# Windowed attention and a squared-ReLU layer on one core: another planned order, and 128-row turns of x for groups 1 to 4

## The chip, the cores and the metric

The kernel runs on one core of one Trainium2 chip. The metric is device time in microseconds of one execution, shown as the median of the timed runs. A profiled execution gives the trace; its span runs from the first to the last instruction.

The engines are named as in the profile: PE is TensorE's matmuls, PEld its loads of weights, DVE is VectorE, ACT ScalarE, POOL GpSimd and SP SyncE. SP does no arithmetic here and only issues DMAs.

## What is computed

Attention in a window of 32 positions to each side, over 8 batches of 8 heads, 576 positions and 64 channels; its result, laid out as 4608 tokens of 512 channels, goes through two matmuls with a squared ReLU between them.

```python
def _attn_ref(q, k, v):                       # each (8, 8, 576, 64)
    scores = (1 / np.sqrt(64)) * np.matmul(q, k.transpose(0, 1, 3, 2))
    mask = np.abs(pos[:, None] - pos[None, :]) <= 32
    scores = np.where(mask, scores, -1e9)
    attn = np.exp(scores - max); attn = attn / (attn.sum(-1) + 1e-9)
    return np.matmul(attn, v)

def _moe_ref(x, w_in, w_out):                 # (4608, 512), (512, 2048), (2048, 512)
    r = np.maximum(x @ w_in, 0.0)
    return (r * r) @ w_out

x = attn_out.transpose(0, 2, 1, 3).reshape(4608, 512)
```

## The kernel before

**Attention, in 24 groups.** A group is 192 positions of one batch with all 8 heads, three groups to a batch; group `G` is `g = G % 3` of batch `b = G // 3`. For each group GpSimd issues loads of q, k and v, which also turn float32 into bfloat16 (`load_qk` at L487, `load_v` at L536; `load_pair` at L519 in batches 0 and 1). Then q and k are turned so that channels lie on partitions: for groups 0 to 5 by matmuls with the identity (`turn_pe`, L578) and an eviction (L606, L609), from group 6 on by DMA transposes on SP (`turn_dma`, L618, four for a group, called `td` in the code).

The scores `S` are L659 in groups 0 to 2 and L707 after that, 24 matmuls with 64 rows. ScalarE takes the exponential (`X`, L721 and L724), VectorE multiplies with the band mask (`M`, L729 and L735), which gives `pt`. Two value products follow, `P{G}A` and `P{G}B` (L763, eight matmuls each). v has a column of ones, so each product also gives the row sums. After the first, VectorE takes the reciprocal (`R`, L782) and multiplies (`N`, L785), which gives 64 rows of x in `xa`; then the place in PSUM is cleared (`Z`, L793 on ScalarE or L795 on VectorE), since the second product adds onto it, and the same steps give 128 rows in `xb`. The 64 rows of `xa` lie on partitions 64 to 127.

**Turning x** (`xturn`). x is needed with channels on partitions, in the ring `xt`. Groups 0 to 4 are turned on TensorE: `T{G}a` turns the 64 rows of `xa` by four transposes of 64 rows (L843), `T{G}b` the 128 rows of `xb` by four of 128 (L848), both into one PSUM bank, and ScalarE evicts both at once (L860). Group 0 has its own code (L813, L818). From group 5 on, two DMA transposes on SP do it (L864, L867).

**The two matmuls.** The up-product `A` (L889) takes blocks of 192 tokens up to token 2304 and of 256 after that, in pieces of eight matmuls. ScalarE applies the ReLU (`r`, L895), and ScalarE or VectorE squares (`g`, L905 or L903) into the ring `gt`. The last 512 tokens go through seven products in place of eight (`mm1_pair`, L966). The down-product runs over pairs of 128 tokens, seven products `P1` to `P7` of eight matmuls each (`mm2_pair`, L1083, with sums formed by VectorE at L1069); the first two blocks go without that (`mm2`, L1023).

**What sets the order.** `Prog.rec` records every operation with its reads and writes, a duration, and a key, which is a place in the order that the code wishes for. `Prog.schedule` then plans time with these numbers: at each step the engine that is free first takes the ready operation with the smallest key, and some may go to either ScalarE or VectorE (`alt`). Keys get random offsets from `SEEDS` within `NOISE`, and offsets for each kind of operation (`OFFS`, `FLEX`). A DMA's planned landing is that of a model of the queues plus a slack: `LSLACK` for loads from batch 2 on, `XSLACK` for turns of x on SP. The plan only fixes the order on each engine; on the chip every operation waits for semaphores. `gate` holds the loads of a group back until a given operation on TensorE is done, from group 12 on the second value product of group `G - 4`. `kind` and `change` charge the plan about 0.1 us where TensorE changes between matmuls of 64 rows and others, and prefer to keep such operations together. Where the plan leaves TensorE free in the opening, matmuls over zeros (L412, "idle") are put in.

```python
def kind(self, op):
    n = op.name
    return "s" if n[0] == "S" or n[0] == "T" and n[-1] == "a" else ...
def change(self, a, b):
    return 0 if a == b else 110 if b == "s" else 100 if a == "s" or b == "t" else 30 if b == "v" else 0
```

## Time and profile before

| what | us |
|---|---|
| median of 3 timed runs | 290.09 |
| the three runs | 293.07, 290.09, 288.38 |
| the profiled execution's own time | 291.74 |
| its span, first to last instruction | 289.9 |
| TensorE busy in the span | 282.1 |
| VectorE / ScalarE / GpSimd busy | 219.8 / 215.4 / 106.8 |

In the rows of the profile the form `128*128 128x256` means 128 rows of weights by 128 columns, and an output of 128 partitions by 256. `xN` is the number of instructions. In the order of time a row begins with start and length in us; the start of the next row is the better measure of how long a stretch of matmuls holds TensorE, since matmuls overlap at their ends. `[0.74 <-DMA xt<-xb]` behind a row is idle time of that engine ahead of it and what ended it.

### The profile page before, as it was taken

To read this page: it belongs to the slowest core of one execution; us is meant where nothing else is said; L and a number is where in the kernel's file an instruction comes from. 1 tells how busy PE (TensorE), PEld (TensorE's weight loads), DVE (VectorE), ACT (ScalarE), POOL (GpSimd) and SP (SyncE) were. 2 spreads that over 40 slices of the span, in tenths; PEclk is the share of its full clock that TensorE was granted. 3 is DMA by queue.
4 is the path that set the end of the run, shared out by engine and by line. 5 is a ranking of instruction groups with operands and counts; after the bars stand their busy time and mean duration, and the time that the engine had idled before them with its cause. 6 is when DMAs were issued, how large, how long until landed. Compare 5 with 4: busy or idle time off the path is not lost.

```text
span 289.9 us, 8460 instructions
## 1 busy us (share of the span) xinstructions
PE 282.1 (97%) x3424; PEld 245.2 (85%) x3430; DVE 219.8 (76%) x472; ACT 215.4 (74%) x404; POOL 106.8 (37%) x143
## 2 busy tenths in 40 slices
PE   7998999999999999999999899999999999999996
PEld 2567988698899999999988788898889888888885
DVE  6668679969668978688866664987898857889863
ACT  3379999985489889688978898777887855788310
POOL 8985663260264664454665246425000000000000
PEclk9999999999999999999999999999999999999999
DMA  9999999999599999999999999999922030202124
GB/s 167 188 194 176 205 179 161 135 195 132 128 158 179 131 165 141 210 150 134 179 145 188 150 122 186 169 152 187 170 41 84 20 102 0 76 0 76 72 75 145
DMA packets 158983, 39.59 MB, mean 137 GB/s; under 512 B 148320, under 2 KB 154592, under 8 KB 158944
## 3 DMA queue, kind: packets, MB, share of 16 engines
q0 software_dynamic: 106016, 17.93, 89.8%
q1 hardware_dynamic: 47888, 12.07, 31.7%
q10 hardware_dynamic: 5040, 9.05, 10.0%
q8 instruction: 27, 0.44, 0.7%
q14 instruction: 12, 0.10, 0.1%
HBM read 36.70 MB, written 9.44 MB: 159 GB/s over the span
## 4 chain that ended last, share of the span: by engine, by line
PE 87%; DMA 5%; DVE 5%; ACT 2%; issue 1%; DVEq 0%
PE ht L889 32%; PE outp L1083 29%; PE at L1083 6%; PE at L763 4%; DMA xt<-xb 3%; PE at L707 3%; PE outp L1023 2%; PE at L966 2%; PE ht L966 2%; DMA oe<-in_q_dram 1%; PE outp L412 1%; PE outp L889 1%; PE at L889 1%; DVE kt L609 1%; PE at L578 1%
## 5 line engine op out<-in xcount | busy, mean ns | idle before, releaser
L889 PE MATMUL ht<-xt,w 128*128 128x192 bf16 (+1 forms) x1120 | 119.5, 256 | 0.7 <-DMA xt<-xb 0.7
L889 PEld LDWEIGHTS ht<-xt,w 128*128 128x128 bf16 x1120 | 96.6, 98 | 8.0 <-DMA xt<-xb 1.0
L895 ACT ACTIVATE rt<-ht 128x384 bf16<-128x384 f32 (+1 forms) x140 | 72.2, 529 | 21.7 <-PE ht L889 20.6
L905 ACT ACTIVATE gt<-rt 128x384 bf16<-128x384 bf16 (+1 forms) x122 | 67.1, 566 | 2.4
L536 POOL DMA_DIRECT2D v<-in_v_dram x48 | 38.3, 805 | 43.8 <-PE at L763 19.4
L487 POOL DMA_DIRECT2D kraw<-in_k_dram x36 | 28.1, 783 | 36.5 <-issue 14.6
L487 POOL DMA_DIRECT2D qraw<-in_q_dram x36 | 28.1, 782 | 10.3 <-PE ht L889 5.2
L1083 PE MATMUL outp<-w,gt 128*128 128x256 bf16 x224 | 29.0, 273 | 0.0
L1083 PE MATMUL outp<-tw,gt 128*128 128x256 bf16 x224 | 29.0, 273 | 0.0
L1083 PE MATMUL outp<-tw,ss 128*128 128x256 bf16 x224 | 28.9, 273 | 0.1
L1083 PEld LDWEIGHTS outp<-w,gt 128*128 128x128 bf16 x224 | 21.5, 98 | 2.6
L1083 PEld LDWEIGHTS outp<-tw,gt 128*128 128x128 bf16 x224 | 21.7, 98 | 2.3
L1083 PEld LDWEIGHTS outp<-tw,ss 128*128 128x128 bf16 x224 | 21.2, 98 | 2.7 <-DVE ss L1069 0.3
L721 ACT ACTIVATE e<-at 128x1024 bf16<-128x1024 f32 x21 | 21.4, 1021 | 2.1 <-PE at L707 1.9
L763 PE MATMUL at<-v,pt 128*128 128x66 bf16 x384 | 20.1, 194 | 0.5 <-DVE pt L735 0.5
L735 DVE TENSOR_TENSOR pt<-em,mask 64x512 bf16<-64x512 bf16 x42 | 17.6, 420 | 3.8 <-ACT em L724 2.4
L763 PEld LDWEIGHTS at<-v,pt 128*128 128x128 bf16 x384 | 17.9, 98 | 1.7 <-DVE pt L735 0.8
L903 DVE TENSOR_TENSOR gt<-rt 128x384 bf16<-128x384 bf16 (+1 forms) x30 | 11.4, 382 | 10.2 <-ACT rt L895 10.0
L729 DVE TENSOR_TENSOR pt<-e,mask 128x1024 bf16<-128x1024 bf16 x21 | 14.5, 691 | 5.4 <-ACT e L721 5.0
L1103 DVE TENSOR_TENSOR oe<-outp,uu 128x256 f32<-128x256 f32 (+1 forms) x28 | 15.4, 551 | 3.4 <-PE outp L1083 2.8
L785 DVE TENSOR_TENSOR xa<-at,rs 64x512 bf16<-64x512 f32 x24 | 16.7, 695 | 1.1
L785 DVE TENSOR_TENSOR xb<-at,rs 128x512 bf16<-128x512 f32 x24 | 16.5, 686 | 0.7
(151 smaller groups left out, 412.0 us busy)
## 6 DMA issues: line engine op xcount, KB each, us to landing
out_dram<-oe ACTq DMA_DIRECT2D x34, 256.0 KB, 4.6
qraw<-in_q_dram POOLq DMA_DIRECT2D x36, 96.0 KB, 7.3
w<-in_moe_w_in_dram POOLq DMA_DIRECT2D x4, 512.0 KB, 11.0
v<-in_v_dram POOLq DMA_DIRECT2D x16, 128.0 KB, 8.1
w<-in_moe_w_out_dram POOLq DMA_DIRECT2D x4, 512.0 KB, 17.6
v<-in_v_dram POOLq DMA_DIRECT2D x16, 96.0 KB, 7.3
kraw<-in_k_dram POOLq DMA_DIRECT2D x12, 112.0 KB, 7.2
kraw<-in_k_dram POOLq DMA_DIRECT2D x12, 96.0 KB, 7.4
```

The costliest lines, as they stand in the source:

```text
L487: self.p.rec("POOL", lambda e, j=j: e.dma_start(raw[0:h, j, :].rearrange("p (h d) -> p h d", h=8), s[:, j]), writes=[("raw", t, G % NRAW, ...
L536: self.p.rec("POOL", lambda e, j=j, lo=lo, hi=hi, k0=k0: e.dma_start(vt[lo - k0:hi - k0, j, :, 0:64], self.v[b, :, lo:hi, :].rearrange("h ...
L721: self.p.rec("ACT", lambda e: e.activation(e2[:], self.AT[:, 0:1024], ACTF.Exp, scale=0.125), reads=lo, writes=[("e", n)], key=key, dur=ac ...
L729: self.p.rec("DVE", lambda e: e.tensor_tensor(out, e2[:].rearrange("p (h s q) -> p h s q", h=8, s=2), mb, ALU.mult), reads=[("e", n), ("ma ...
L735: self.p.rec("DVE", lambda e, w=w, r=r, x=x, mm=mm: e.tensor_tensor(pt[x:x + 64, w, :, 0:64], e1[r:r + 64, :].rearrange("p (h q) -> p h q" ...
L763: mm = e.matmul(avp[:, c:c + VS], pt[:, 4 * (h % 2) + h // 2, :], vt[:, w, h, :], start=(w == 0 and y == 0), stop=True, skip_group_check=True)
L785: self.p.rec("DVE", lambda e: e.tensor_tensor(x[r0:128, :].rearrange("p (x y c) -> p x y c", x=2, y=4), av[:, :, :, 0:64], rb, ALU.mult), ...
L889: mm = e.matmul(ht[:, n * x:n * x + n], self.W1[:, ft, 128 * d:128 * d + 128], self.XT[:, ft, r:r + n], start=(ft == 0), stop=(ft == 3))
L895: self.p.rec("ACT", lambda e: e.activation(rt[:, 0:c], ht[:, 0:c], ACTF.Relu), reads=htag, writes=[("rt", k % 4)], key=key, dur=act(c), na ...
L905: alt=("ACT", lambda e: e.activation(gt[:, d0:d0 + len(ds), r:r + n], rr, ACTF.Square), act(c), "g")
L1083: mm = e.matmul(op[:, 256 * half:256 * half + 256], a[:, d, :], w[:, d, :], start=first and d == 0, stop=d == 7, skip_group_check=True)
L1103: self.p.rec("DVE", lambda e: e.tensor_tensor(out, src, other, ALU.add), reads=btags[bank] + rd, writes=wr, key=key + k * PSTEP - DLEAD, d ...
```

## The change

Three things change in the program. First, the planner's numbers: more slack for turns of x on SP (3200 to 4200 ns) and for loads (1200 to 1600 ns), other seeds with more noise, other offsets of keys, down-products later (`LAGP`), and two entries of the opening's list of loads exchanged. Second, `T1a` to `T4a`: the transposes of `xa` take all 128 rows of it, of which the first 64 are zeros, and write 128 columns; `T{G}b` and the eviction shift by 64 columns. Third, three operations fill the zero rows of the three `xa` buffers once, at the head of the program. The planner no longer counts `T1a` to `T4a` among the 64-row matmuls. `KPL` and `LAGS` are 0, so the code that they bring stays unused.

```diff
-XSLACK = 3200
-LSLACK = 1200
+XSLACK = 4200
+LSLACK = 1600
-NOISE = 0.1
+NOISE = 0.4
-LAGP = 14.0
+LAGP = 15
+TFULL = True
...
-        return "s" if n[0] == "S" or n[0] == "T" and n[-1] == "a" else ...
+        return "s" if n[0] == "S" or n[0] == "T" and n[-1] == "a" and (not TFULL or n == "T0a") else ...
...
+            c = 64 * TFULL
             def f0(e):
                 for j in range(4):
-                    mm = e.transpose(ps[:, 192 * j:192 * j + 64], xa[64:128, 128 * j:128 * j + 128], self.ID[64:128, 64:128])
+                    mm = e.transpose(ps[:, 192 * j:192 * j + 128], xa[:, 128 * j:128 * j + 128], self.ID[:])
             def f1(e):
                 for j in range(4):
-                    mm = e.transpose(pb[:, 192 * j + 64:192 * j + 192], xb[:, 128 * j:128 * j + 128], self.ID[:])
+                    mm = e.transpose(pb[:, 192 * j + 64 + c:192 * j + 192 + c], xb[:, 128 * j:128 * j + 128], self.ID[:])
...
-            self.p.rec("PE", f0, reads=[("xa", G % 3), "id"], writes=bank, key=key, dur=110, name=f"T{G}a")
+            self.p.rec("PE", f0, reads=[("xa", G % 3), "id"] + [("xz", G % 3)] * TFULL, writes=bank, key=key, dur=110, name=f"T{G}a")
...
-                                                     ps[:, 0:768].rearrange("p (j q) -> p j q", j=4), ACTF.Copy),
+                                                     ps[:, c:768 + c].rearrange("p (j q) -> p j q", j=4), ACTF.Copy),
...
+        for i in range(3 * TFULL):
+            x = self.XA[i][0:64, :]
+            at(-20, lambda i, x: self.p.rec("DVE", lambda e: e.memset(x, 0.0), reads=["zz"], writes=[("xz", i)], key=XZKEY + i, dur=200, name=f"xz{i}",
+                                            alt=("ACT", lambda e: e.activation(x, self.ZZ[0:64, :], ACTF.Copy), 490, "Z")), i, x)
```

The new order on the engines shows at three places. A row is a run of equal instructions; `at` is the PSUM tensor of attention, `ht` that of the up-product, `outp` that of the down-product.

The first place is TensorE around the turn of x of group 1. Before, from its second value product (first row):

```order
L763 MATMUL at<-v,pt 128x66 x8
L659 MATMUL at<-qt,kt 128x128 x8
L889 MATMUL ht<-xt,w 128x192 x8
L843 MATMUL at<-ident,xa 128x64 x4
L848 MATMUL at<-ident,xb 128x128 x4
L889 MATMUL ht<-xt,w 128x192 x8
```

The same place in the changed kernel, whose lines have moved (L767 for L763, L663 for L659, L898 for L889, L850 and L857 for the turns):

```order
L767 MATMUL at<-v,pt 128x66 x8
L663 MATMUL at<-qt,kt 128x128 x8
L850 MATMUL at<-ident,xa 128x128 x4
L857 MATMUL at<-ident,xb 128x128 x4
L898 MATMUL ht<-xt,w 128x192 x16
```

Both turns have moved ahead of an up-product piece that used to stand before them.

The second place is TensorE between the two value products of group 6. Before, with L763 at both:

```order
L763 MATMUL at<-v,pt 128x66 x8
L1083 MATMUL outp<-w,gt 128x256 x8
L1083 MATMUL outp<-tw,ss 128x256 x16
L1083 MATMUL outp<-tw,gt 128x256 x8
L763 MATMUL at<-v,pt 128x66 x8
```

And in the changed kernel, where L767 is the value product and L1092 the down-product:

```order
L1092 MATMUL outp<-tw,ss 128x256 x16
L767 MATMUL at<-v,pt 128x66 x8
L1092 MATMUL outp<-tw,gt 128x256 x8
L1092 MATMUL outp<-w,gt 128x256 x8
L767 MATMUL at<-v,pt 128x66 x8
```

Four products of the down-product stood between them, and two stand there now.

The third place is TensorE in groups 7 and 8, from the first value product of group 7 to that of group 8 (the third L763); L707 are the scores of group 8. Before:

```order
L763 MATMUL at<-v,pt 128x66 x8
L889 MATMUL ht<-xt,w 128x192 x16
L1083 MATMUL outp<-w,gt 128x256 x8
L889 MATMUL ht<-xt,w 128x192 x8
L763 MATMUL at<-v,pt 128x66 x8
L889 MATMUL ht<-xt,w 128x192 x16
L707 MATMUL at<-qt,kt 128x64 x24
L889 MATMUL ht<-xt,w 128x192 x16
L1083 MATMUL outp<-tw,ss 128x256 x8
L889 MATMUL ht<-xt,w 128x192 x16
L763 MATMUL at<-v,pt 128x66 x8
```

In the changed kernel, L711 being the scores:

```order
L767 MATMUL at<-v,pt 128x66 x8
L898 MATMUL ht<-xt,w 128x192 x24
L767 MATMUL at<-v,pt 128x66 x8
L898 MATMUL ht<-xt,w 128x192 x16
L711 MATMUL at<-qt,kt 128x64 x24
L898 MATMUL ht<-xt,w 128x192 x24
L767 MATMUL at<-v,pt 128x66 x8
```

Between the two value products of group 7 the same three up-product pieces stand without the down-product among them; between the scores and the first value product of group 8 stand three pieces, where four and a down-product were.

More of the change, by code (lines that the diff above doesn't have):

```diff
@@ L29 @@
 GD = 3
-GK = 7.0
+GK = 6.5
 TDKEY = 5.0
@@ L35 @@
 TBK = 0
+TFULL = True
+XZKEY = -5
+LAGS = 0.0
+KPL = 0
 GDL = 1
@@ L161, in kind @@
         n = op.name
-        return "s" if n[0] == "S" or n[0] == "T" and n[-1] == "a" else "t" if n[0] == "t" else "v" if n[0] == "P" and "." not in n else ""
+        return "s" if n[0] == "S" or n[0] == "T" and n[-1] == "a" and (not TFULL or n == "T0a") else "t" if n[0] == "t" else "v" if n[0] == "P" and "." not in n else ""
     def change(self, a, b):
@@ L1242, in build @@
                 at(t0 / 64 - 2, self.mm1_tile, t0, t0 / 64 + MOE)
-                for d in range(8):
-                    at(t0 / 64 + d + MOE, self.mm1_pair, t0, d, t0 / 64 + d + MOE)
+                for y in range(2):
+                    for d in range(0, KPL, 2):
+                        for d0 in (d, 8 + d):
+                            key = t0 / 64 + d / 2 - 2 + 0.2 * (d0 > 7) + MOE if y == 0 else t0 / 64 + 8 - KPL / 2 + d / 2 + 0.2 * (d0 > 7) + MOE
+                            at(key, self.mm1, t0 + 256 * y, 256, [d0, d0 + 1], key)
+                for d in range(KPL, 8):
+                    key = t0 / 64 + d - KPL / 2 + MOE
+                    at(key, self.mm1_pair, t0, d, key)
                 t0 += 512
```

25 lines of the change are left out of this document (14 added, 11 removed), and 2 rows, old and new, of the table OPENING.

## The prediction

> **What bounds the kernel now.** I read the page first, for the share of each engine and for the groups of instructions, then the list of TensorE's waits, then the order of time on TensorE.
>
> ```profile
> span 289.9 us, 8460 instructions
> PE 282.1 (97%) x3424; PEld 245.2 (85%) x3430; DVE 219.8 (76%) x472; ACT 215.4 (74%) x404; POOL 106.8 (37%) x143
> ```
>
> The program has one core, and its TensorE (PE) computes for 282.1 of 289.9 us. The other engines have about a quarter of their time free. A gain can only come from TensorE's list itself or from its 7.8 us without work. These are told by two more views: the list of what TensorE waited for, with total, count and longest in us, and a table by stage.
>
> ```profile
> PE at L843 <- DVE xb L785: 0.8, 1, 0.8
> PE ht L889 <- DMA xt<-xb: 0.7, 1, 0.7
> ...
> PE at L763 <- DVE pt L735: 0.5, 1, 0.5
> ...
> 0.00:2.00 2.00, 0.81 (x2) 0.28 (x3) 1.14 (x9) 1.25 (x1) 1.02 (x6) 1.00 0.03 10
> 2.00:30.00 28.00, 25.77 (x283) 16.82 (x284) 20.20 (x57) 17.30 (x29) 22.69 (x30) 1.00 1.60 194
> ...
> 287.00:290.00 3.00, 0.14 (x2) 0.00 (x0) 0.52 (x2) 0.00 (x0) 0.00 (x0) 0.97 0.59 206
> ```
>
> The first column of a stage after its length is TensorE's busy time, and the third number from the end the granted clock, which is full. Of the 7.8 us, 1.2 lie ahead of the first matmul, 2.2 in the opening up to 30 us, 2.8 behind the last matmul. In the 257 us between there are only two waits worth a name, 0.7 us on a turned block of x (`DMA xt<-xb`) and 0.5 us on a masked tile (`DVE pt`). So everything after the opening is a TensorE stream with almost no holes. A new order can take away the 1.2 us of these two, fractions of the opening, and whatever the matmuls themselves cost less. It can put new waits anywhere.
>
> **The 128-row turn.** Turning x of groups 1 to 4 keeps its matmul count; four of each group read 128 rows instead of 64. Group 4 in the order of time on TensorE:
>
> ```profile
> 55.10 1.03 PE L1023 MATMUL outp<-w,gt 128*128 128x512 bf16 x4
> 56.06 0.29 PE L843 MATMUL at<-ident,xa 64*128 64x64 bf16 x4
> 56.28 0.40 PE L848 MATMUL at<-ident,xb 128*128 128x128 bf16 x4
> 56.51 1.03 PE L1023 MATMUL outp<-w,gt 128*128 128x512 bf16 x4
> 57.38 0.38 PE L1083 MATMUL outp<-w,gt 128*128 128x256 bf16 x2
> ```
>
> From start to start, four 512-column matmuls take 57.38 - 56.51 = 0.87 us. The ones that start at 55.10 would be over at 55.97, and the 64-row turn starts at 56.06: 0.09 us pass ahead of it. The turn itself takes 56.28 - 56.06 = 0.22 us, the 128-row turn behind it 0.23. A 128-row turn in place of the 64-row one therefore saves 0.09 - 0.01 = 0.08 us, in four groups 0.3 us; if what lies within the 0.22 us is also partly a change of shape, up to 0.1 us more in each, 0.7 in all. I take **-0.4 us**, between 0 and -0.7. The Trainium skill speaks to both sides of this. Its page "TensorEngine Tiling (Array Packing)", section "Key Properties", says that a change of the tiling mode drains TensorE, and the 0.09 us agree. Its page "TensorE: Matmul & The Clock Gate", section "Back-to-back issue gap", speaks against the change: it gives about 25 ns for up to 64 columns and N/2.4 + 2.5 ns, 56 ns, at 128. By that, sixteen matmuls would cost an estimated 0.5 us more and eat the gain, and the sum below would end 0.4 us higher; the 0.22 and 0.23 us of the two turns do not bear it out.
>
> The three zero fills stand at the head of ScalarE's list (the order shows `xa<-zz` there). ScalarE is idle then, and they are hidden unless they last longer than this wait:
>
> ```profile
> 4.95 0.63 ACT L507 ACTIVATE qraw<-oe 96x512 bf16<-96x512 f32 x1 [2.92 <-DMA oe<-in_q_dram]
> ```
>
> Three copies of 512 elements at no more than that row's 0.63 us are 1.9 us out of 2.92: **0**. Without that cover each would put 0.6 us ahead of the first turned q.
>
> **The opening.** Three idle matmuls fewer (32 to 29 in the order) are no gain where the next real work still waits for a load; at 1.02/4 us, by the first row below, they bound it at -0.8. Work does move at the first turn of x:
>
> ```profile
> 16.42 1.02 PE L412 MATMUL outp<-zz 128*128 128x512 bf16 x4
> 24.60 0.42 PE L763 MATMUL at<-v,pt 128*128 128x66 bf16 x8
> 24.95 0.40 PE L659 MATMUL at<-qt,kt 64*128 64x128 bf16 x8
> 25.28 0.83 PE L889 MATMUL ht<-xt,w 128*128 128x192 bf16 x8
> 26.87 0.29 PE L843 MATMUL at<-ident,xa 64*128 64x64 bf16 x4 [0.75 <-DVE xb L785]
> 27.09 0.40 PE L848 MATMUL at<-ident,xb 128*128 128x128 bf16 x4
> 79.00 0.82 PE L889 MATMUL ht<-xt,w 128*128 128x192 bf16 x8
> 79.66 0.42 PE L763 MATMUL at<-v,pt 128*128 128x66 bf16 x8
> 26.12 0.68 DVE L785 TENSOR_TENSOR xb<-at,rs 128x512 bf16<-128x512 f32 x1
> ```
>
> VectorE finishes xb at 26.80, and the turn starts 0.07 us later. Before, one up-product piece (L889 x8, 0.66 us, as from 79.00 to 79.66) stands ahead of both turns; in the change it stands behind them, and only the turn of xa (0.23) may run ahead. TensorE would have nothing to do from 24.60 + 0.35 + 0.33 + 0.23 = 25.51 to 26.87, 1.36 us in place of the 26.87 - 25.94 = 0.93 of now: +0.43. VectorE also gives an eviction of kt to ScalarE there and gets a square instead, so xb can come somewhat earlier; by the 0.68 us of its own row at most, which would turn the +0.43 into -0.25. I take **+0.4**, between -0.8 and +0.9.
>
> **The two waits in the stream.**
>
> ```profile
> 160.40 1.92 PE L889 MATMUL ht<-xt,w 128*128 128x256 bf16 x16 [0.74 <-DMA xt<-xb]
> 181.54 0.43 PE L763 MATMUL at<-v,pt 128*128 128x66 bf16 x8 [0.48 <-DVE pt L735]
> 78.13 1.04 PE L1083 MATMUL outp<-tw,gt 128*128 128x256 bf16 x8
> ```
>
> The first is group 14's xb. In the change two more pieces of eight 256-column matmuls (from 78.13 to 79.00, 0.87 us each) stand between its second value product and the up-product that reads it: 1.7 us more cover for 0.7 us of wait. What is late next is then xa of group 13, whose cover shrinks by 1.4 us. The second wait keeps its distance from its scores and hangs on VectorE's backlog; I count half of it. Together **-1.0**, between -1.2 and 0.
>
> **New short distances at groups 6 to 8.** Two chains have a least length, which the trace shows. From scores to the first value product (group 7) and from first to second value product (group 12):
>
> ```profile
> 76.34 0.53 PE L707 MATMUL at<-qt,kt 64*128 64x64 bf16 x24
> 76.80 1.49 PE L889 MATMUL ht<-xt,w 128*128 128x192 bf16 x16
> 78.45 0.69 DVE L729 TENSOR_TENSOR pt<-e,mask 128x1024 bf16<-128x1024 bf16 x1
> 125.66 0.42 PE L763 MATMUL at<-v,pt 128*128 128x66 bf16 x8
> 127.29 0.61 ACT L793 ACTIVATE at<-zz 64x528 f32<-64x528 bf16 x1
> 128.11 0.42 PE L763 MATMUL at<-v,pt 128*128 128x66 bf16 x8
> ```
>
> The mask is done at 79.14, 2.80 us after the scores begin; the value product can follow 0.07 us later, as the turn above did. In the change group 8 has only three up-product pieces there: 0.46 + 3 x 0.66 = 2.44 us, short by 0.43. The second chain is 128.11 - 125.66 = 2.45 us with the clearing on ScalarE, where the change has it for both groups. Group 6 now has 0.26 + 2 x 0.87 = 2.00 us there, short by 0.45; group 7 has 0.26 + 3 x 0.66 = 2.24, short by 0.21. Sum **+1.1**. It is at least 0 if the waits fall into each other, and 2.5 if VectorE is 0.5 us behind at each.
>
> **Loads.** Counted along the order with the durations above, the operation that lets the loads of group 10 go stands 21.1 us of TensorE work ahead of its scores, before 26.6; groups 9 and 11 lose 5.0 and 4.5, groups 13 to 23 gain up to 2.6. Group 10's loads from issue, and the DMA transposes that turn them:
>
> ```profile
> L487 POOL DMA_DIRECT2D kraw<-in_k_dram x2: 772/786/799, 78.0 to 81.9; - x2
> DMA to landing us min/median/max: 3.8/7.3/8.0
> L618 SPq DMA_TRANSPOSE kt<-kraw x3: 1204/1255/1929, 87.1 to 93.6; - x3
> DMA to landing us min/median/max: 4.9/5.6/7.2
> ```
>
> Last issue 3.9 us after the first, 7.3 to land, 1.3 for an issue on SP, 5.6 to land: 18.1 us by medians, 20.4 by the longest. It fits into 21.1, so **0**; but 0.7 us are left in the bad case, and SP's row also holds the turns of x. I bound it at +2. It does not add up over the groups: these loads are let go ahead of group 9's scores, so a wait there gives the next ones time.
>
> **Sum.** -0.4 + 0.4 - 1.0 + 1.1 + 0 = +0.1 us on the profiled span of 289.9. That execution took 291.74 us, 1.84 of it around the span; the three timed runs are 288.38, 290.09 and 293.07, so it lies within their spread. On the median I forecast **290.2 us**, no change.
>
> **Rivals.** *All of the slack is real* (0.25): the short distances at groups 6 to 8 fall into one another, and the removed waits go for good: -0.4 - 1.2 - 0.7 = -2.3, **287.8 us**. For it: the order has more cover where the only DMA wait was. Against it: three distances lie below chains that the trace shows. *Loads late* (0.12): scores of groups 9 to 12 wait for kt or qt. It decides once a load and its transpose take over 21.1 us together; with 2 us of lateness and one repetition behind group 12's own gate this is +3 and, with the +0.1, **293.2 us**, slower. Against it: by the medians 3.0 us are left. *VectorE behind* (0.13): the order gives VectorE 40 of the squares of the up-product instead of 30, at the 0.38 us of the row below 3.8 us more, and masks and normalisations queue behind them. Waits of 0.48 us, like that at 181.54, at six more places are +2.9 and make **293.1 us**. Against it: in the whole trace TensorE waited for a mask only once.
>
> ```profile
> L903 DVE TENSOR_TENSOR gt<-rt 128x384 bf16<-128x384 bf16 (+1 forms) x30 | 11.4, 382 | 10.2 <-ACT rt L895 10.0
> ```
>
> **How the numbers follow.** The forecast itself has 0.50. About 2% (5.8 us) is what a measurement of this kernel can tell from no change. For a faster result by that much all holes of the stream and the opening would have to go and more; 0.02. Slower by it needs two of the slower rivals at once; 0.05. The rest, 0.93, is within. The range takes in the faster rival less 1 us for the spread of the runs, and both slower ones: 286.8 to 293.6 us.
>
> **What would show it.** Right: ahead of the 128-row turns of groups 2 to 4 no 0.09 us, and TensorE's waits hold entries of 0.2 to 0.5 us at the value products of groups 6, 7 and 8 and one over 1 us at the turn of xb of group 1, none on `DMA xt<-xb`. Wrong: scores (L707's successor) that wait for a DMA, or value products that wait for `DVE pt` beyond group 8, or a span under 287.

## The result, and the profile after

The changed kernel takes **294.63 us** (median of 4 runs, 292.6 to 295.23), the kernel before beside it 290.08; the ratio is 1.0159, with a 95% interval from 1.0121 to 1.0198. Measured again on other chips the change came out at 292.19 us against 288.76, a ratio of 1.0113 [1.0079, 1.0148], and, with a few idle copies at its end, at 292.65 against 289.64, 1.0089 [1.0051, 1.0127]. By the medians the change costs between 3.0 and 4.6 us. Ratios and their intervals leave out the executions that ran more than 1.5% above a kernel's fastest; medians and ranges keep them. The forecast was no change, 286.8 to 293.6 us.

The page of the changed kernel, for the profiled execution of 295.17 us:

```profile
span 292.9 us, 8452 instructions
PE 281.1 (96%) x3422; PEld 244.8 (84%) x3427; DVE 222.5 (76%) x482; ACT 211.8 (72%) x397; POOL 107.4 (37%) x143
```

TensorE is busy for 1.0 us less than before and the span is 3.0 us longer: what was lost is mostly waiting, and a short stretch in which TensorE ran slower and counts as busy. Some of the waits of TensorE, with total, count and longest in us:

```profile
PE at L767 <- DVE at L799: 1.4, 1, 1.4
PE at L850 <- DVE xb L789: 1.4, 1, 1.4
...
PE ht L898 <- issue: 0.9, 1, 0.9
...
PE ht L898 <- ACT rt L904: 0.7, 1, 0.7
```

The second entry is the turn of x of group 1, which I had forecast. The first, third and fourth I had not. The first and third lie close together, in the order of time on TensorE:

```profile
178.32 0.42 PE L767 MATMUL at<-v,pt 128*128 128x66 bf16 x8
...
179.45 1.91 PE L1092 MATMUL outp<-tw,ss 128*128 128x256 bf16 x16
182.80 0.41 PE L767 MATMUL at<-v,pt 128*128 128x66 bf16 x8 [1.44 <-DVE at L799]
184.09 2.76 PE L898 MATMUL ht<-xt,w 128*128 128x256 bf16 x16 [0.88 <-issue]
187.05 1.67 PE L1092 MATMUL outp<-w,gt 128*128 128x256 bf16 x8 [0.20 <-DVE uu L1112]
188.65 0.52 PE L711 MATMUL at<-qt,kt 64*128 64x64 bf16 x24
```

The two value products of group 18 stand at 178.32 and 182.80. The second waits 1.44 us for VectorE's clearing of its PSUM place. The up-product behind it waits another 0.88, and the view names no releaser (`issue`). By the kernel that piece reads the turned xa of group 17, whose transpose SP issues here:

```profile
175.81 1.20 SPq L873 DMA_TRANSPOSE xt<-xa  x1
```

It landed 8.2 us later, at 184.00, and the up-product starts at 184.09. The down-product at 187.05 waits 0.20 for the sum `uu` of VectorE, and its eight matmuls take 1.60 us to the next row, where eight of that shape took 0.87 before. VectorE at the same time:

```profile
177.38 0.68 DVE L733 TENSOR_TENSOR pt<-e,mask 128x1024 bf16<-128x1024 bf16 x1
179.99 0.69 DVE L931 TENSOR_TENSOR kraw<-w 128x1024 bf16<-128x1024 bf16 x1 [1.92 <-issue]
180.71 0.21 DVE L786 RECIPROCAL rs<-at 64x8 f32<-64x8 f32 x1
...
182.15 0.50 DVE L799 MEMSET at<- 64x528 f32 x1 [0.18 <-DVE xa L789]
185.68 0.69 DVE L931 TENSOR_TENSOR kraw<-kraw,w 128x1024 bf16<-128x1024 bf16 x1 [3.03 <-DMA kt<-kraw]
186.41 0.21 DVE L786 RECIPROCAL rs<-at 128x8 f32<-128x8 f32 x1
```

L931 (L922 before) is in `setup_w1s`: eight sums of the first layer's weights, with which the last 512 tokens do with seven products in place of eight. They are called `ws00`, `ws01`, `ws10` and so on; the two here are `ws01` and `ws10`. They are not urgent, and the kernel gives them no buffers of their own: they are written into raw buffers of k and q that are no longer needed. They have to wait until the DMA transposes that read such a buffer have landed. VectorE takes its list in order. In the changed order `ws01` stands right ahead of the first reciprocal of group 18 and `ws10` right ahead of the second, and both of them stand there and wait, 1.92 and 3.03 us. Behind `ws01` are queued the reciprocal, the normalisation and the clearing, over at 182.65, for which the value product waits; behind `ws10` the second reciprocal and `uu`, for which the down-product waits. For `ws01` the view names no DMA, but the last transpose of k of group 19 landed at 179.91, 0.08 us ahead of it.

Before, `ws10` stood a group later (at 191.31, without a wait). `ws01` waited as well, ahead of the mask of group 18:

```profile
176.14 0.41 DVE L903 TENSOR_TENSOR gt<-rt 128x512 bf16<-128x512 bf16 x1
179.74 0.69 DVE L922 TENSOR_TENSOR kraw<-w 128x1024 bf16<-128x1024 bf16 x1 [3.18 <-issue]
180.34 0.68 DVE L729 TENSOR_TENSOR pt<-e,mask 128x1024 bf16<-128x1024 bf16 x1
```

That is the origin of the 0.48 us at 181.54 which I had put down to VectorE's backlog: VectorE had nothing to do for 3.18 us and was held up by one instruction, until the last transpose of k of group 19 landed at 179.66.

Why the sums stand where they do follows from the planner. It lets `ws10` begin at the very moment at which, by its model, the last transpose of k of group 20 lands, 7.8 us after that transpose starts its issue; in the trace the landing came 8.6 us after the issue. That is 0.8 of the 3.03 us. The rest is that the issue itself came late against VectorE's list: 5.6 us ahead of the end of the clearing that precedes `ws10`, where the plan has 7.6. Why it came late is not shown. In the plan of before the same sum had 2.4 us to spare and `ws01` none, and `ws01` is the one that waited there; in the plan of the change `ws01` has 1.7 us to spare, and it waited all the same. I first put the move down to the constant `WLEAD`, which the change raises from 3 to 6.5; planned with 3 and all else as in the change, the list has both sums in the same places, so it comes from the new plan as a whole.

To see where the rest went, I summed up TensorE's work ahead of each row of its order, with the same lengths for all kernels (0.66 us for eight up-product matmuls of 192 columns, 0.87 for eight of 256, and so on), and subtracted this from the row's start. Where the difference grows, TensorE waited or was slow. Its growth in us, by stretches of TensorE's work, for the profiled executions:

| stretch of TensorE's work | before | change, 1st | change, 2nd | change, 3rd |
|---|---|---|---|---|
| 10 to 30 us (turns of x of groups 1 to 3) | 1.17 | 1.45 | 1.45 | 1.45 |
| 30 to 50 (turn of group 4) | -0.07 | -0.27 | -0.26 | -0.26 |
| 50 to 90 (groups 6 to 9) | 0.47 | 1.68 | 1.67 | 1.67 |
| 90 to 150 | 0.81 | -0.01 | -0.01 | -0.01 |
| 150 to the end (group 18) | 0.65 | 4.65 | 1.48 | 0.31 |
| own time less span | 1.84 | 2.27 | 2.21 | 2.29 |

The first three rows repeat to 0.02 us in the three profiles of the change. What varies is the stretch with group 18, and, ahead of 10 us of work, the opening, which differs by 0.7 us between these three and by 2 us between executions of the order of before, and is left out here. The profile of before is one of its slow openings: a row of seven matmuls over zeros there takes 3.19 us, 3.13 in the kernel with the new turns alone, and 1.68 in four other profiles of kernels made from the order of before. In these four the row at 10 us of work comes 12.3 to 12.8 us late, and 12.3 to 13.0 in the eight profiles with the changed order: the opening ahead of it does not tell the orders apart. The last row is the time of an execution outside its span: 1.75 to 1.88 us in every run of the order of before, 2.19 to 2.32 in every run of the changed order.

The growth at group 18 comes in steps. In the first profile they are 1.6 us at the value product (behind `ws01`), 1.0 at the up-product (the turned block of x), and 1.9 from there to the scores at 188.65, of which the wait on `uu` (behind `ws10`) is 0.2 and the rest the slower TensorE of the last section. In the second they are 0.7 (the turned block) and 0.8 (behind `ws10`), in the third 0.3 (behind `ws10`). Waits in a row hide one another: without the turned block's the one behind `ws10` would have been longer.

### The profile page after: what moved, and what is told of

It reads as the page before. It is cut to its first block, busy times and chain, and to the rows that moved or that the text cites. A ratio compares the mean times of both kernels' runs of the same rounds, so it can differ in the third digit from the quotient of the medians.

```text
span 292.9 us, 8452 instructions
## 1 busy us (share of the span) xinstructions
PE 281.1 (96%) x3422; PEld 244.8 (84%) x3427; DVE 222.5 (76%) x482; ACT 211.8 (72%) x397; POOL 107.4 (37%) x143
## 4 chain that ended last, share of the span: by engine, by line
PE 84%; DMA 5%; DVE 4%; ACT 4%; issue 1%; SPq 0%; DVEq 0%
PE ht L898 32%; PE outp L1092 28%; PE at L1092 6%; PE at L767 4%; PE at L711 3%; DMA kt<-kraw 3%; PE outp L1032 2%; PE ht L975 2%; PE at L975 2%; DMA oe<-in_k_dram 2%; ACT rt L904 2%; PE outp L898 1%; PE at L898 1%; DVE kt L613 1%; PE at L582 1%
## 5 line engine op out<-in xcount | busy, mean ns | idle before, releaser
L898 PE MATMUL ht<-xt,w 128*128 128x192 bf16 (+1 forms) x1120 | 119.3, 257 | 2.4 <-issue 0.9
L898 PEld LDWEIGHTS ht<-xt,w 128*128 128x128 bf16 x1120 | 96.8, 98 | 9.5 <-issue 1.1
L914 ACT ACTIVATE gt<-rt 128x384 bf16<-128x384 bf16 (+1 forms) x112 | 62.2, 567 | 2.7 <-ACT rt L904 0.2
L1092 PE MATMUL outp<-w,gt 128*128 128x256 bf16 x224 | 29.7, 277 | 0.2 <-DVE uu L1112 0.2
L1092 PE MATMUL outp<-tw,gt 128*128 128x256 bf16 x224 | 29.0, 273 | 0.0
L1092 PE MATMUL outp<-tw,ss 128*128 128x256 bf16 x224 | 27.9, 273 | 0.0
L1092 PEld LDWEIGHTS outp<-w,gt 128*128 128x128 bf16 x224 | 21.8, 99 | 3.5 <-ACT gt L914 0.6
L912 DVE TENSOR_TENSOR gt<-rt 128x384 bf16<-128x384 bf16 (+1 forms) x40 | 15.1, 378 | 11.8 <-ACT rt L904 11.2
L1092 PEld LDWEIGHTS outp<-tw,ss 128*128 128x128 bf16 x224 | 21.6, 98 | 2.4
L1092 PEld LDWEIGHTS outp<-tw,gt 128*128 128x128 bf16 x224 | 21.5, 98 | 2.4
L767 PE MATMUL at<-v,pt 128*128 128x66 bf16 x384 | 20.1, 194 | 1.5 <-DVE at L799 1.4
L767 PEld LDWEIGHTS at<-v,pt 128*128 128x128 bf16 x384 | 17.7, 98 | 3.6 <-issue 2.5
```

The costliest lines, as they stand in the source:

```text
L767: mm = e.matmul(avp[:, c:c + VS], pt[:, 4 * (h % 2) + h // 2, :], vt[:, w, h, :], start=(w == 0 and y == 0), stop=True, skip_group_check=True)
L898: mm = e.matmul(ht[:, n * x:n * x + n], self.W1[:, ft, 128 * d:128 * d + 128], self.XT[:, ft, r:r + n], start=(ft == 0), stop=(ft == 3))
L912: self.p.rec("DVE", lambda e: e.tensor_tensor(gt[:, d0:d0 + len(ds), r:r + n], rr, rr, ALU.mult), reads=[("rt", k % 4)], writes=wr, key=ke ...
L914: alt=("ACT", lambda e: e.activation(gt[:, d0:d0 + len(ds), r:r + n], rr, ACTF.Square), act(c), "g")
L1092: mm = e.matmul(op[:, 256 * half:256 * half + 256], a[:, d, :], w[:, d, :], start=first and d == 0, stop=d == 7, skip_group_check=True)
```

## The experiments

Operations keep their lists but for single moves. A pair `(name, ahead)` takes an operation out of its engine's planned order and puts it ahead of another one; nothing else changes, and the semaphores follow the data:

```python
for name, ahead in MOVES:
    op = self.named[name]
    self.ops.remove(op)
    self.ops.insert(self.ops.index(self.named[ahead]), op)
```

In the names `P18B` is the second value product of group 18, `N`, `R`, `Z` the steps on VectorE, `A960.10` an up-product piece, `P4.4` the fourth product of the down-product of blocks 4 and 5. Theory A says that the two sums ahead of the reciprocals of group 18 make the loss. Its rival is that it comes from the other moves, above all the short distances on TensorE.

### Both sums late, and one alone

```diff
+MOVES = (("ws01", "N18B"), ("ws10", "R19A"))     # both late, in the changed order
+MOVES = (("ws10", "R19A"),)                      # ws10 alone
```

Expected of both sums late: 

> The changed kernel, its order kept on all engines but for two of VectorE's eight sums of first-layer weights (L931): the second and the third stand later, beside the normalisations of groups 18 and 19. Theory A: the loss is that VectorE, which takes its list in order, stands at these two until the DMA transposes of k of groups 19 and 20 have landed (1.9 and 3.0 us in the profile), and the second value product of group 18 behind it. Then the order costs nothing else: 290.5 us, and no wait of TensorE over 0.5 us between 150 and 250 us. Rival B, ten more squares on VectorE keep it behind: 293.5 to 295, with the value products waiting for it elsewhere. Rival C, scores of groups 18 to 20 wait for their own transposes: 293 to 294, with TensorE's wait at the scores.

Expected of `ws10` alone: 

> The changed kernel with only the third sum of weights moved behind the second value product of group 19. Theory A: the 3.0 us wait goes, the 1.9 us wait at the second sum stays; most of the loss is the first, 291 to 292 us. Rivals B and C: 293 to 295.

Measured beside before at 289.15 us: both late 291.56 us, ratio 1.0103 [1.0039, 1.0167]; `ws10` alone late 291.86 us, 1.0083 [1.0043, 1.0123]. In both profiles the waits near 182 us are gone, and from 150 us of work to the end the lateness grows by 0.1 us in place of 4.65. Of `ws01` the pair says nothing: in the profile with `ws10` alone late it stands where the change has it and does not wait, so the 1.9 us expected there did not come. The up-product's wait is gone as well, though no sum is ahead of it: with `ws10` alone late, group 17's turned xa landed at 180.99, in time for the start at 181.22. And a loss of some 2.5 us stays, with no wait behind 86 us. Theory A holds for a part of the stall and not for the whole.

### The early sum in the order of before

```diff
+MOVES = (("ws10", "R18B"),)                      # in the order of before
```

> The kernel before, with one operation of VectorE moved: the third sum of weights (L922) stands ahead of the reciprocal behind the second value product of group 18, as the change has it, instead of one group later. Theory A: VectorE then stands there until about 189.7 us, when the last transpose of k of group 20 landed in the profile of before, 4 to 5 us; what TensorE has to do meanwhile hides part of it, so 292 to 294 us. Rivals B and C know nothing of this operation: 290.

Measured: 295.49 us (294.77 to 298.2), ratio 1.0218 [1.0178, 1.0257]. One operation of 0.69 us in another place on VectorE goes with a loss of about 6 us, more than the 292 to 294 us expected. In the list of TensorE's waits stand

```profile
PE ht L898 <- DMA xt<-xb: 3.2, 1, 3.2
PE at L716 <- DVE xb L794: 2.7, 1, 2.7
```

The second is the sum, which held up xb of group 18 and, behind it in VectorE's list, all that followed. The first, at 161.77, is not: it is group 14's xb, which before made TensorE wait 0.74 us and here 3.24. It lies ahead of the moved operation, and I have no cause for its growth. The profiled execution is the slowest of the five, 298.2 us; these two waits and two stretches at half clock (last section), at an estimated 1.7 us each, are 9.4 of its 10.0 us above the lowest run of before, 288.18. How the 6 us of the median divide is not shown.

### The 128-row turns alone

```diff
-                    mm = e.transpose(ps[:, 192 * j:192 * j + 64], xa[64:128, 128 * j:128 * j + 128], self.ID[64:128, 64:128])
+                    mm = e.transpose(ps[:, 192 * j:192 * j + 128], xa[:, 128 * j:128 * j + 128], self.ID[:])
...
```

This is the order of before with the new turns and the zero fills and nothing else. 

> The kernel before with its order kept on every engine, and only the turns of x of groups 1 to 4 by 128-row matmuls over zeros, with the three zero fills ahead of ScalarE's list. By the rows of before: 0.3 to 0.4 us faster, 289.7 us, no 0.09 us ahead of the turns of groups 2 to 4. By the count of columns alone it would be 0.5 us slower, 290.5.

Measured: 288.66 us (287.72 to 291.7), ratio 1.0 [0.9971, 1.003]. The turns are no part of the loss. In its profile neither the wait on `xt<-xb` at group 14 nor the one at group 18 appears, though nothing in that part of the program had changed: from 90 us of work to the end the lateness grows by -0.1 us where the profile of before has 1.46. Both of before's waits in the stream hang on the execution, not on the order alone: in six profiles of before and of kernels made from its order the wait at group 14 shows in two (0.74 and 3.24 us), and of the five that leave `ws01` in its place it waits in one.

### The change again

> The changed kernel itself, unaltered, run beside the others on one chip. Theory A (two of the eight sums of first-layer weights, ws01 and ws10, now stand in VectorE's list ahead of the reciprocals of group 18 and wait there for DMA transposes of groups 19 and 20): about 294.3 us, and again a wait of over 1 us of TensorE at the second value product of group 18 and VectorE rows of the sums with waits of 2 to 3 us at about 180 and 185 us. Theory B (the loss is spread over the new order, and the place near 185 us is one of several that differ from run to run): the same time but no such wait in this profile, or a wait elsewhere of the same size.

Measured: 292.19 us, ratio 1.0113 [1.0079, 1.0148]. In VectorE's order of time the sums wait again, but less, and TensorE's second value product at 180.33 does not wait at all:

```profile
177.49 0.69 DVE L931 TENSOR_TENSOR kraw<-w 128x1024 bf16<-128x1024 bf16 x1 [0.29 <-issue]
...
182.46 0.69 DVE L931 TENSOR_TENSOR kraw<-kraw,w 128x1024 bf16<-128x1024 bf16 x1 [2.30 <-DMA kt<-kraw]
```

```profile
180.33 0.42 PE L767 MATMUL at<-v,pt 128*128 128x66 bf16 x8
181.31 1.91 PE L898 MATMUL ht<-xt,w 128*128 128x256 bf16 x16 [0.56 <-issue]
183.82 1.03 PE L1092 MATMUL outp<-w,gt 128*128 128x256 bf16 x8 [0.60 <-DVE uu L1112]
```

The place costs 1.48 us here, without half clock. The 0.56 are again the turned xa of group 17, which landed at 181.22; the 0.60 stand behind `ws10`. I had expected over 1 us at the value product; what waits here, and for how long, is not fixed but hangs on when the transposes land.

### The sum late, and the change with copies at its end, on one chip

```diff
+        last = max(i for i, o in enumerate(self.ops) if o.eng == "ACT")
...
+            self.ops.insert(last + 1, w)         # eight copies of 8 elements on ScalarE
```

`ws10` late: 

> The changed order with ws10 alone moved late, again, now on one chip with the changed order itself (padded at its end). Theory A in its size from the undisturbed second profile of the changed kernel: 1.3 to 1.5 us below the changed order; from the first profile, with the half clock: 4 us below. The span less than the own time by 2.2 us, as in all runs of this order.

The change with copies at the end of ScalarE's list: 

> The changed kernel with eight small copies at the very end of ScalarE's list, behind its last copy and ahead of nothing, so that ScalarE has as many instructions as before (405 for 404, where the change has 397). The own time of the execution exceeds the span by 1.81 us in every run of the order of before and by 2.24 in every run of the changed order. If that hangs on the number of ScalarE's instructions (a fetch of instructions fewer, 11 for 12), the difference falls to 1.8; if not, it stays at 2.2. The span itself is that of the changed order, 288.6 to 291.8 us.

Measured beside before at 289.64 us: `ws10` late 291.13 us, 1.0068 [1.0037, 1.0100]; the change 292.65 us, 1.0089 [1.0051, 1.0127]. The medians lie 1.5 us apart, but the intervals of the ratios overlap. Over the executions that the ratios count the means lie 1.1 us apart, with a 95% interval from 0.1 to 2.1: the early `ws10` costs something, and its size is poorly known. In the third profile of the change its wait is shorter still:

```profile
181.73 0.69 DVE L941 TENSOR_TENSOR kraw<-kraw,w 128x1024 bf16<-128x1024 bf16 x1 [1.43 <-issue]
182.46 0.21 DVE L796 RECIPROCAL rs<-at 128x8 f32<-128x8 f32 x1
```

The transpose that it waits for landed 8.6, 7.3 and 6.0 us after its issue in the three profiles, `ws10` waited 3.03, 2.30 and 1.43 us, and the place, with the other waits there, cost TensorE 4.65, 1.48 and 0.31; with the sum late 0.1 in all three profiles. Own time less span stayed at 2.22 to 2.29 us in spite of the copies: it does not hang on ScalarE's number of instructions. But the copies did not change what the expectation had in mind. One DMA queue of the kind `instruction` moves 12 packets in all six profiles of before and of kernels made from its order, and 11 in all eight with the changed order, the one with the copies included. So this rival stays untested:

```profile
q14 instruction: 12, 0.10, 0.1%
q14 instruction: 11, 0.09, 0.1%
```

What makes these 0.43 us is open.

### The short distances

```diff
+MOVES = (("ws01", "N18B"), ("ws10", "R19A"), ("A0.12", "T1a"), ("A960.10", "P7B"))
```

This is the changed order with both sums late and one up-product piece put back ahead of the turn of x of group 1, another ahead of `P7B`. 

> The changed order with both sums late, and two up-product pieces put back ahead of operations that they used to cover: one ahead of the turn of x of group 1, one ahead of the second value product of group 7. If the short distances cost what the trace shows (1.44 us of wait instead of 0.93 at the turn of group 1, about 0.3 us at the second value product of group 7), the time is 0.5 to 0.8 us below that of the same order without these two moves, which was 1.010 of before: 1.008 of before, some 290.8 to 291.2 us where before is 289.2. If what is left of the loss lies in the opening's warm-up of the clock or in other places, no difference from 1.010.

Measured: 292.99 us, 1.0112 [1.0079, 1.0146], no gain. At the turn of group 1 two waits of 0.80 and 0.49 us took the place of one of 1.44, the first of them on a load of weights (`DMA w<-in_moe_w_in_dram`), which the piece put earlier now meets; at groups 7 and 8 three of 0.6 to 0.7 came. And at the up-product of the tokens from 2816 on TensorE waited for a turned block of x, as it had once in before:

```profile
170.33 1.03 PE L907 MATMUL ht<-xt,w 128*128 128x256 bf16 x8 [1.84 <-DMA xt<-xb]
...
183.68 1.91 PE L907 MATMUL ht<-xt,w 128*128 128x256 bf16 x16 [0.26 <-issue]
```

The second row is the up-product that reads the turned xa of group 17, which landed at 183.59: with both sums late it waits again, so this wait is not theirs.

At groups 7 and 8 distance was not what was missing. What was missing, TensorE and ScalarE show in the second profile of the change, each in the order of time:

```profile
82.39 0.53 PE L711 MATMUL at<-qt,kt 64*128 64x64 bf16 x24
82.85 1.49 PE L898 MATMUL ht<-xt,w 128*128 128x192 bf16 x16
85.06 0.83 PE L898 MATMUL ht<-xt,w 128*128 128x192 bf16 x8 [0.72 <-ACT rt L904]
85.73 0.42 PE L767 MATMUL at<-v,pt 128*128 128x66 bf16 x8
```

```profile
82.75 0.47 ACT L904 ACTIVATE rt<-ht 128x384 bf16<-128x384 f32 x1
83.12 0.59 ACT L728 ACTIVATE em<-at 128x512 bf16<-128x512 f32 x1
83.60 1.03 ACT L725 ACTIVATE e<-at 128x1024 bf16<-128x1024 f32 x1
84.51 0.88 ACT L904 ACTIVATE rt<-ht 128x384 bf16<-128x384 f32 x2
```

Behind the scores of group 8 ScalarE takes both exponentials, 83.12 to 84.51, and no ReLU meanwhile. The up-product has two PSUM banks; both are full at 84.2, and the third piece waits until the ReLU behind the exponentials has read the first, at 85.06. Before, a product of the down-product stood at that place, which needs neither bank. That the value product then comes 3.34 us after the scores, more than the 2.80 that I had counted, is a consequence: the missing cover was short for two chains, and the other one was longer.

Two kernels tried the place itself. One is the changed order with `ws10` late and TensorE's order of groups 7 and 8 put back nearly as it was; the other is the order of before with the new turns and TensorE's order of groups 7 and 8 as in the change:

```diff
+MOVES = (("ws10", "R19A"), ("A960.4", "P7A"), ("P4.4", "A960.4"), ("P1.6", "P7B"), ("A1152.4", "P8A"))
+MOVES = (("P4.4", "S7B"), ("P1.6", "A960.0"), ("P7A", "A960.4"), ("P7B", "A960.10"), ("S8B", "A960.14"), ("P8A", "P5.6"), ("P5.6", "A1152.8"))
```

The first: 

> The changed order with ws10 late and TensorE's order of groups 7 and 8 almost as it was before: a product of the down-product again behind the scores of group 7 and another between its two value products, and one up-product piece more between the scores and the first value product of group 8. Nothing else moves. Theory: nine up-product pieces in a row, without a down-product among them, run ahead of ScalarE's ReLU, and the last waits 0.7 to 0.9 us for its PSUM bank; with the small waits of 0.1 to 0.2 us at the value products this place costs 1.2 us. Then this kernel is 0.9 to 1.3 us below the one with ws10 late alone, and the wait on the ReLU near 85 us is gone from its profile. Rival: ScalarE is behind there whatever TensorE's order is, and the wait shows up at the next piece; no difference.

The second: 

> The order of before with the 128-row turns, which alone gave 1.000 of before, and TensorE's order of groups 7 and 8 as in the change: no down-product between the scores of group 7 and the first value product of group 8, where two stood. The other engines' orders are those of before. Theory (nine up-product pieces in a row run ahead of ScalarE's ReLU): a wait of TensorE of 0.6 to 0.9 us on the ReLU at about 85 us, small waits at the value products, and 0.8 to 1.2 us more than without it, 1.003 to 1.004 of before. Rival: in before's order ScalarE has more squares behind it and the wait is larger, up to 2 us. Second rival: the down-products that come later fill the hole, and no difference.

Measured: 293.25 us, 1.0122 [1.0079, 1.0165], and 291.76 us, 1.0090 [1.0056, 1.0125]. Both are slower than the kernels that they were made from, by 2.1 us against the one with `ws10` late on the same chip, and by 0.9% against an order that had shown 1.0. Their waits are of another kind, here in TensorE's order of time in the first and in the list of TensorE's waits in the second:

```profile
79.66 0.83 PE L914 MATMUL ht<-xt,w 128*128 128x192 bf16 x8 [2.22 <-ACT rt L920]
...
87.15 1.08 PE L914 MATMUL ht<-xt,w 128*128 128x192 bf16 x11 [0.76 <-ACT rt L920]
```

```profile
PE at L779 <- DVE pt L751: 1.9, 1, 1.9
...
PE at L779 <- DVE at L811: 1.0, 1, 1.0
```

In the first, ScalarE's next ReLU starts only at 79.11; ahead of it in ScalarE's list stand two output DMAs of the block whose product, `P4.4`, I had moved later. The wait at group 8 stays at 0.76 with two down-products ahead of it, but none between the scores and the third piece: there are not too many up-product pieces in a row, as I had expected, but too few products that need no ReLU behind the exponentials. In the second, masks and the clearing stand in VectorE's list behind squares and sums of pieces that now come later. The lists of the other engines were planned for TensorE's old order, and one list can't be exchanged alone. The price of groups 6 to 9 by itself therefore rests on the table, where it is 1.2 us in all three profiles of the change, and not on an experiment.

### A try at a faster kernel

```diff
+MOVES = (("ws01", "R18A"), ("A0.14", "T1a"))     # order of before, 128-row turns
```

> The order of before with the 128-row turns, which alone gave 1.000 of before, and two moves: ws01 behind the mask of group 18 instead of ahead of it, and one up-product piece put ahead of the turn of x of group 1. Theory A says that before's own stall of 0.5 us at the first value product of group 18 comes from ws01, which waits 3.2 us there for a transpose, and not from a backlog of VectorE: the stall goes, and TensorE's list of waits has no entry on a masked tile there; with up to 0.7 us at the turn of x of group 1 the time is 0.5 to 1.0 us below before, 0.997 of it. If VectorE's backlog makes the stall, it stays and the time is that of before. If ws01 in its new place delays the reciprocal of group 18 in turn, a wait of about as much at the second value product of group 18 and no gain.

Measured: 288.66 us (288.24 to 290.43), 1.0002 [0.9983, 1.0020]. `ws01` behind the mask does not wait, and no value product waits there; since the kernel without the move had not waited there either in its profile, this says little. The wait at the turn of group 1 only split up into 0.55, 0.38 and 0.35 us, the first again on that load of weights. No version beats the kernel before.

### Zeros in the stall

```diff
+        for k in range(12):                      # ahead of S19B
...
+            w.eng, w.fn, w.dma, w.deps, w.i = "PE", self.keep, None, {self.idle_on}, 0
...
```

This is the order of before with `ws10` early and twelve matmuls over zeros where TensorE had waited. 

> The order of before with ws10 early (which alone gave 1.022 of before, with two stretches of 3.41 us at half clock behind TensorE waits of about 3 us), and twelve matmuls of 512 columns over zeros ahead of the second half of the scores of group 19, so that TensorE has some 2.6 us of work where it waited. They add nothing to the result. If the half clock follows from TensorE's standing idle, the profile has no half clock near 190 us and the time falls by up to 1.7 us against the same order without them, to about 1.016 of before; if the half clock comes from something else (the time in the program, the load), it stays and the time is the same or up to 2.6 us longer.

Measured: 292.72 us, 1.0157 [1.0104, 1.0209], where the same order without them had 1.0218 [1.0178, 1.0257] on another chip; the mean granted clock is 1.0 in three of four runs, where it was 0.994 or 0.988 in all five. Behind the stall TensorE runs at full speed:

```profile
183.24 2.75 PE L427 MATMUL at<-zz 128*128 128x512 bf16 x12
187.31 0.52 PE L723 MATMUL at<-qt,kt 64*128 64x64 bf16 x24 [1.31 <-DVE xb L801]
187.76 1.05 PE L1099 MATMUL outp<-w,ss 128*128 128x256 bf16 x8
```

As far as these nine runs show, the half clock follows from TensorE's standing idle. How much of the 2.8 us between the two kernels it is remains open, since the wait at group 14 was missing in this profile too. The early `ws10` keeps the scores waiting from 183.24 to 187.31 here, about the 4.0 us by which the kernel is slower than before.

## Why the prediction was wrong, step by step

**Two steps failed.** One is the account of the change part by part: it followed TensorE's order and the loads, and had no term for VectorE's list, where two instructions that wait for a DMA had moved ahead of ones that TensorE waits for. In the three profiles of the change this is worth about 1.8, 0.8 and 0.3 us, in the first with up to 1.7 us of slower clock on top; by times, 1.1 us for `ws10` on one chip. The other is the term of -1.0 (next paragraph). With one sum or both late the medians still lie 1.5 to 2.7 us above before. The forecast without the -1.0, and with the 0.43 that was missing outside the span, would have been 1.5 above it.

The rival of VectorE being behind named the right engine with the wrong mechanism: it counted 40 squares in place of 30, while what held VectorE up was an empty wait. My list of signs came near: it had value products beyond group 8 that wait for a mask of VectorE, and the one that came waited for its clearing.

**The two waits in the stream, -1.0,** were no gain. The order of before with the new turns runs without both, two of the six profiles have the first, and one of the five with `ws01` in its place has the second. A single profiled execution had supplied the price, and its cause at group 18 was read wrongly: `ws01`, not a backlog. Another wait of this kind came in its place: the prediction looked for the next late block at xa of group 13, and in three of the eight profiles with the changed order it was xa of group 17, with 0.3 to 0.9 us.

**The 128-row turns, -0.4,** were right. From the turn of group 1 to the scores behind the turn of group 4 TensorE takes 31.48 and 31.49 us in the order of before with the 64-row turns (before, and with zeros in the stall), and 31.07 and 31.17 with the 128-row ones (the turns alone, and groups 7 and 8 as in the change): 0.3 to 0.4 us less, too little for the times to show (1.0 [0.9971, 1.003]). One reading was too simple. The four transposes of the 64-row turn of group 4 start 0.04, 0.03 and 0.03 us apart and the next turn 0.12 later, while those of 128 rows start 0.06 apart. So the shorter gap that the prediction held against the change is there, and the change of shape on both sides of it costs more. Group 4 of the changed kernel has no pause ahead of the turn, and 128 rows take as long as 64 did:

```profile
55.55 1.04 PE L1092 MATMUL outp<-w,gt 128*128 128x256 bf16 x8
56.42 0.39 PE L850 MATMUL at<-ident,xa 128*128 128x128 bf16 x4
56.64 0.39 PE L857 MATMUL at<-ident,xb 128*128 128x128 bf16 x4
56.87 1.36 PE L1092 MATMUL outp<-tw,ss 128*128 128x256 bf16 x11
```

From start to start the product takes its 0.87 us, and the turns 0.22 and 0.23.

**The opening, +0.4,** was right: TensorE waits 1.4 us ahead of the turn of group 1, where 1.36 was forecast, and the table's first row grows by 0.49 against the kernel with the turns alone (0.96). Against before it grows by 0.28, since it also holds what the turns of groups 2 and 3 save.

**Groups 6 to 8, +1.1,** came out right in size, 1.2 us, by luck, since the places are wrong: 0.1 at group 6 where 0.45 was forecast, 0.2 to 0.3 at `P7B`, and 0.88 at an up-product piece of group 8 that waits for a ReLU, a chain which I had not looked at.

**The loads, 0,** were right; no scores wait for a DMA in the profiles of the change.

**Outside the span** I had taken 1.84 us for both kernels. It is 0.43 more in the changed order.

With the terms as measured, a quiet execution of the change should lie 0.5 (opening), -0.4 (turns), 1.2 (groups 6 to 9), 0.4 (outside) and at least 0.3 (behind `ws10`) above before, 2.0 us. The lowest times of the change, 290.84 and 290.49, are 2.4 and 2.3 above the lowest of before beside them, 288.43 and 288.22. The rest of the difference of medians is not shown to come from one place. The landings at group 18 are a part of it, but with `ws10` late, too, the medians lie 0.7 and 1.8 us above the lowest run.

## What to carry to other kernels

On an engine that works in order, look in the new order for every instruction that waits for a DMA, and name what is queued behind it, however small and unimportant the instruction is itself. Where a view names no releaser, compare the wait's end with the landings of what the instruction reads and overwrites. Filler work in borrowed buffers belongs behind the urgent work, not at the planned landing of a transfer. Price a wait that is to be removed from several executions, because one that comes from a DMA's landing may be there in one and absent in the next. And where the lists of several engines were planned together, as here, putting back one of them alone need not show what it was worth: both tries here came out slower.

## What the runs showed of the hardware

The granted clock falls for 3.41 us at a time, and not after every wait. The rows below give the length of a stretch, the busy time of TensorE in it and, third from the end, the granted clock. They are laid on the steps of 3.413 us at which the clock changes, of the first profile of the change and of before with `ws10` early:

```profile
181.56:184.97 3.41, 1.29 (x17) 1.13 (x18) 0.91 (x2) 0.00 (x0) 1.35 (x2) 1.00 1.81 223
184.97:188.39 3.42, 3.23 (x17) 2.04 (x15) 2.64 (x6) 1.82 (x3) 3.29 (x5) 0.50 1.57 173
```

```profile
188.38:191.79 3.41, 0.68 (x27) 0.41 (x24) 2.20 (x5) 0.60 (x1) 3.41 (x5) 1.00 1.77 138
191.79:195.20 3.41, 3.41 (x23) 2.41 (x18) 2.56 (x6) 1.51 (x2) 0.12 (x1) 0.50 2.23 159
```

And of the kernel with two distances put back, at its wait of 1.84 us:

```profile
168.31:171.72 3.41, 1.57 (x21) 1.30 (x20) 1.15 (x4) 1.50 (x4) 0.29 (x1) 1.00 1.74 112
171.72:175.13 3.41, 3.41 (x40) 3.08 (x38) 2.63 (x6) 3.14 (x6) 0.00 (x0) 1.00 1.90 151
```

Where TensorE was busy for 1.29 us of such a step or less (0.87 and 0.68 in the other kernel), the next one ran at half clock; where it was busy for 1.57, or for 1.51 in the kernel with groups 7 and 8 put back, it did not. In one step of 3.41 us at half clock an estimated 1.7 us of work are lost. So, by the same estimate, a stall of some 2 us can cost 2 or nearly 4, by how it falls on the steps. The Trainium skill, page "TensorE: Matmul & The Clock Gate", section "Part 1: The HAM clock gate", gives the step as a free-running window of about 3.4 us, and the trace agrees with its 3.413. It puts the fall of the clock behind at least one idle window; here the windows ahead of it were not idle, but busy for 0.68 to 1.29 us.
